# Pooled attention and a maxout layer on one core: more tiles by seven products, and one written order for all engines

## The chip, the core and the metric

The kernel runs on one core of a Trainium2 chip. The metric is device time in microseconds (us), the time of one execution on the device. The profile is of one execution; its times count from the first instruction (the span). The core has five engines that run side by side, each through its own instructions in order: PE (matrix products; PEld are its weight loads), DVE (elementwise work), ACT (activations and copies), POOL (here sums, and the issue of loads) and SP (which here only issues DMAs). PE's results go to PSUM, which the kernel divides into eight banks of 512 float32 columns; the other data lie in SBUF.

## What is computed

```
q, k, v: (8 batches, 8 heads, 576, 64)       pool = 8, so 72 pooled keys
k_p, v_p = means of k and v over 8 neighbours in the sequence
scores   = q @ k_p.T / 8 ;  attn = softmax(scores) ;  o = attn @ v_p
x        = o as 4608 tokens x 512
h        = max(x @ w1, x @ w2, x @ w3)        512 -> 768
out      = h @ w_out                          768 -> 512
```

The output is float32; the products run on 16-bit operands.

## The kernel before

Three algebraic steps stand in both kernels. The kernel subtracts w1 from w2 and w3 (`sub_w`), so that h = x·w1 + max(0, x·(w2−w1), x·(w3−w1)). It multiplies w1 by w_out once (`turn_w`, `linear`, L349), so that the x·w1 part becomes x·wm in the output product. And where it says "by seven products", a product of two matrices, each cut in 2x2 quarters, is made from seven products of quarters instead of eight, with sums of the operands' quarters made before them and sums of the results after them.

The 4608 tokens are worked in nine tiles of 512 (tile 0 to tile 8, `LAST` = 8). Each tile has a first layer (x to h) and an output product (x and h to out). A batch holds 576 tokens, so tiles and batches don't coincide. For each batch:

- q, k and v are loaded by DMA from POOL's queue (`load_q`, L100; `load_k`, L79; `load_v`, L87 and L91). q, k and v of batches 1 and 2 are loaded at the start, later ones two batches ahead, into two buffers each.
- k is summed over 8 neighbours in three steps (`fold_steps`, L161, L162, L164), for batch 1 on DVE and later on POOL, then transposed on PE and put into `kz` (`turn_k`, L199 and L208). v is summed in the same three steps on POOL, into `vp_all`.
- q is transposed: batches 0 to 2 on PE (`turn_q`, L192), batches 3 to 7 by one DMA transpose from SP's queue (step "T", L302).
- scores are one PE step and one exponential on ACT each: `scores` for eight heads of 576 columns (batches 1 to 6), `scores_flat` in nine pieces of 512 columns (batch 7) (L218, L223).
- values (`values`): eight small matmuls into `pav` (L268), a reciprocal and a product on DVE (L274, L276). The result is transposed into `xT`, on PE for batches 0 to 2 (L259), and by DMA from SP's queue from batch 3 on (`turn_x`, L253).

First layer: tiles 0 to 5 directly (`hidden_part`, groups of four matmuls, L362; a relu on ACT, L368; a maximum on DVE, L370). Tiles 6, 7 and 8 by seven products (`seven`, L789), three column groups a, b and c of seven products each, with evictions on ACT (L795, L799) and sums on DVE (L766, L769).

Output: tiles 0, 1, 5 and 6 directly (`project`: per 128 tokens four matmuls L412 and six L416, one ACT copy L421, two stores L425). Tiles 2, 3, 4, 7 and 8 by seven products (`out_seven`, ten matmuls each, L713; ACT copies L723, DVE additions L726, stores L662). The sums of the weights are made by `fold_w` and `fold_out` (L536, L545, L597), of x by `sums_of` (L612) and `fold_x` (L564), of h by `sums_of` and `fold_h` (L628).

The order is written out by hand, as lists of step names that the program runs through; every engine executes its share of the steps in the order in which they are written. `block(0, ...)` does tile 0 with batches 0 and 1 woven in; `MIDDLE` does tiles 1 to 4, with the batch after next's loads and sums; `block(5, LEAD, ...)` does tile 5; `ORDER`, through `weave`, does the rest but the last output. In these lists "s3" is the third head's scores, "v2" a value chunk of 128 tokens, "x2" its transpose, "k" the keys, "h" half a first-layer group, "1" to "7" (or "o1" to "o7") output products, "1a" to "7c" seven-product steps of a first layer, "F" half an output tile. In `MIDDLE`, "!" makes the next POOL sum wait for the last DVE sum of two SBUF operands (`gate`, `held`, `after`).

PSUM is divided three times: pools `ps0` (start), `psp` (tiles 0 to 5: `att` twice two banks, `tr` one, `pw` three), and `psq` (the rest).

## Time and profile before

| what | value |
|---|---|
| times of three runs | 226.16, 233.84 and 234.19 us, median 233.84 |
| the profiled execution | 228.01 us, of which the span is 226.3 us |
| DVE, ACT and POOL busy | 148.6, 122.3 and 138.6 us |
| PE, matmuls | 1807 |
| DMA | 33.54 MB; 195 GB/s of HBM traffic over the span |
| L362, first layers directly | 336 matmuls |
| L789 and L713, seven products | 252 and 350 matmuls |
| POOL sums of v, first step (L161) | 7, 4061 ns each |
| POOL sums of k, first step (L161) | 6, 3125 ns each |
| qT by DMA (L302) | 5, median 7.0 us from issue to landing |
| loads of q, k and v, 576 KB each | medians 13.0, 8.2 and 17.5 us from issue to landing |

How to read the profile: each line of groups names a source line, an engine, an operation, what it writes and reads ("out<-in"), its shape, its count, its busy time and the mean time of one, and then the idle time of its engine ahead of it with what ended it. A PE record lasts longer than the time for which it keeps the next matmul away, since matmuls overlap; from one matmul's start to the next one's start is the better measure. In a table of windows each row is a stretch of the span with the busy time and the count of instructions of PE, PEld, DVE, ACT and POOL, the granted TensorE clock, the DMA share and the DMA rate.

### The profile page before, as it was taken

The numbers are of one execution on the slowest core, as the hardware profiler recorded it, in microseconds if no ns is written. First come the engines' busy times: TensorE is split into PE (matmuls) and PEld (weight loads), VectorE is DVE, ScalarE is ACT, GpSimd is POOL, SyncE is SP. The second block draws the span as 40 slices with busy tenths as digits, with TensorE's granted clock in tenths as the row PEclk, the third lists the DMA queues.
The fourth block names the chain that finished last, engine by engine and source line by source line (L and its number), as shares of the span: only waits on it lengthen the run. The fifth ranks groups of instructions, "written<-read, shape, count | busy, mean of one in ns | idle before, by whom it ended". The sixth has DMA issues, their size and how long they took to land.

```text
span 226.3 us, 4691 instructions
## 1 busy us (share of the span) xinstructions
PE 214.7 (95%) x1807; PEld 146.4 (65%) x1807; DVE 148.6 (66%) x292; ACT 122.3 (54%) x221; POOL 138.6 (61%) x111
## 2 busy tenths in 40 slices
PE   6788999999999999999999999699999999999993
PEld 2467745558656555965686568355677677788882
DVE  3668876038595385876679668535668886898840
ACT  2267524755874577238624862475687446555330
POOL 7974300999949967787677758999500913872020
PEclk9999999999999999999999999999999999999999
DMA  6999999989759999659999599965241534200265
GB/s 167 210 197 197 208 207 208 203 163 224 128 106 191 217 220 208 112 129 151 199 226 191 31 216 236 182 126 132 58 107 29 122 61 95 46 3 0 55 203 164
DMA packets 47351, 33.54 MB, mean 148 GB/s; under 512 B 27041, under 2 KB 42337, under 8 KB 47329
## 3 DMA queue, kind: packets, MB, share of 16 engines
q0 software_dynamic: 16944, 16.98, 48.1%
q1 hardware_dynamic: 29936, 15.87, 33.0%
q10 hardware_dynamic: 448, 0.39, 0.7%
q8 instruction: 14, 0.23, 0.5%
q14 instruction: 9, 0.07, 0.1%
HBM read 34.60 MB, written 9.44 MB: 195 GB/s over the span
## 4 chain that ended last, share of the span: by engine, by line
PE 69%; DMA 15%; POOL 11%; issue 1%; DVE 1%; ACT 1%; POOLq 0%
PE pw L362 21%; PE oA L713 9%; DMA vt<-in_v_dram 8%; PE pA L789 7%; PE po L416 7%; PE po L412 5%; PE oC L713 4%; PE psc L218 4%; DMA mw<-in_moe_w_dram 4%; PE pC L789 3%; POOL half L161 3%; DMA xT<-xn 3%; PE pav L268 3%; PE oB L713 2%; POOL half L162 2%; PE pB L789 2%
## 5 line engine op out<-in xcount | busy, mean ns | idle before, releaser
L362 PE MATMUL pw<-xT,mw 128*128 128x512 f16 (+1 forms) x336 | 72.8, 348 | 1.9 <-DMA xT<-xn 1.6
L362 PEld LDWEIGHTS <-mw 128*128 128x128 f16 x336 | 31.6, 98 | 22.3 <-DMA xT<-xn 1.8
L370 DVE TENSOR_TENSOR hT<-t,pw 128x512 f16<-128x512 f16 (+1 forms) x42 | 25.4, 609 | 25.1 <-ACT et L223 17.8
L223 ACT ACTIVATE et<-psc 72x576 f16<-72x576 f32 (+2 forms) x54 | 35.2, 661 | 6.8 <-PE psc L218 6.7
L161 POOL TENSOR_TENSOR half<-vt 72x2048 f32<-72x2048 f16 x7 | 28.4, 4061 | 13.8 <-DMA vt<-in_v_dram 13.3
L162 POOL TENSOR_TENSOR half<-half 72x1024 f32<-72x1024 f32 (+1 forms) x13 | 27.3, 2098 | 11.0 <-DVE rcp L274 6.1
L368 ACT ACTIVATE t<-pw 128x512 f16<-128x512 f32 (+1 forms) x42 | 22.5, 537 | 16.2 <-PE pw L362 15.8
L276 DVE TENSOR_TENSOR xn<-pav,rcp 128x512 f16<-128x512 f32 x40 | 27.7, 692 | 1.4
L416 PE MATMUL po<-mwo,hT 128*128 128x512 f16 (+1 forms) x102 | 23.5, 366 | 0.0
L218 PE MATMUL psc<-qT,kz 128*128 128x320 bf16 (+2 forms) x120 | 22.4, 278 | 0.8 <-DVE qT L194 0.6
L218 PEld LDWEIGHTS <-kz 128*128 128x128 bf16 x143 | 13.1, 98 | 13.3 <-ACT qT L194 1.1
L161 POOL TENSOR_TENSOR half<-ktFalse 96x1536 f32<-96x1536 f16 x6 | 18.7, 3125 | 4.0 <-issue 2.9
L564 POOL TENSOR_TENSOR pad<-xT 128x256 f16<-128x256 f16 x8 | 5.9, 732 | 22.5 <-ACT pad L795 13.9
L795 ACT CAST pad<-pA 128x512 f16<-128x512 f32 x27 | 15.6, 588 | 7.2 <-PE pA L789 7.0
L268 PEld LDWEIGHTS <-et 72*128 72x128 f16 x320 | 15.1, 98 | 3.6 <-issue 0.4
L723 ACT COPY osb<-oA 128x512 f32<-128x512 f32 x12 | 7.0, 586 | 19.2 <-PE oA L713 19.2
L274 DVE RECIPROCAL rcp<-pav 128x8 f32<-128x8 f32 x40 | 8.2, 204 | 14.0 <-PE pav L268 13.6
L412 PE MATMUL po<-wm,xT 128*128 128x512 f16 (+1 forms) x68 | 16.6, 366 | 0.0
L268 PE MATMUL pav<-vp,et 72*128 72x65 f16 x320 | 16.4, 194 | 0.1
L421 ACT COPY osb<-po 128x512 f32<-128x512 f32 (+1 forms) x16 | 9.2, 573 | 12.0 <-PE po L416 12.0
L789 PEld LDWEIGHTS <-sw 128*128 128x128 f16 x144 | 13.7, 98 | 2.5
L766 DVE TENSOR_TENSOR pad<-pad,pC 128x512 f16<-128x512 f16 x18 | 12.3, 685 | 3.9 <-PE pC L789 3.6
(122 smaller groups left out, 380.0 us busy)
## 6 DMA issues: line engine op xcount, KB each, us to landing
out_dram<-osb SPq DMA_DIRECT2D x38, 128.0 KB, 5.5
ktFalse<-in_k_dram POOLq DMA_DIRECT2D x7, 576.0 KB, 8.2
qb<-in_q_dram POOLq DMA_DIRECT2D x7, 576.0 KB, 13.0
vt<-in_v_dram POOLq DMA_DIRECT2D x7, 576.0 KB, 17.5
mw<-in_moe_w_dram POOLq DMA_DIRECT2D x9, 256.0 KB, 9.4
out_dram<-osb SPq DMA_DIRECT2D x8, 256.0 KB, 7.4
ktTrue<-in_k_dram SPq DMA_DIRECT2D x3, 384.0 KB, 5.2
out_dram<-ob SPq DMA_DIRECT2D x8, 128.0 KB, 2.6
```

The source lines that it names most:

```text
L161: yield e.tensor_tensor(out=f, in0=t[:, :, 0:4, :], in1=t[:, :, 4:8, :], op=ALU.add)
L162: yield e.tensor_tensor(out=f[:, :, 0:2, :], in0=f[:, :, 0:2, :], in1=f[:, :, 2:4, :], op=ALU.add)
L218: nc.tensor.matmul(out, kz_all[b % 2][f % 2][rows, h, :], qTs[b][rows, n + i0:n + i1, 64 * (h % 2):64 * (h % 2) + 64], start=True, stop=True)
L223: nc.scalar.activation(out=out, in_=in_, func=FT.Exp, scale=1.0 / 64.0)
L268: nc.tensor.matmul(pav[:, h // 4, 65 * (h % 4):65 * (h % 4) + 65], ets[b][:, h, c0:c0 + 128], vp_all[:, b, h, :], start=True, stop=True)
L276: nc.vector.tensor_tensor(out=xn, in0=pv[:, :, :, 0:D], in1=rcp.to_broadcast([128, 2, 4, D]), op=ALU.mult)
L362: mm = nc.tensor.matmul(pw, w_sb[wi][:, kc, bass.ts(jc, 128)], x[:, kc], start=(kc == 0), stop=(kc == KCH - 1))
L370: nc.vector.tensor_tensor(out=hT[:, jc, c0:c1], in0=t, in1=pw, op=ALU.max)
L412: nc.tensor.matmul(po, tokens(128 * m, 128 * m + 128)[:, kc], wm_sb[:, kc, c], start=(kc == 0), stop=False)
L416: nc.tensor.matmul(po, hT[:, jc, bass.ts(mm, 128)], wo_sb[:, jc, c], start=False, stop=(jc == JCH - 1))
L713: nc.tensor.matmul(p, left, right, stop=(r == 4), skip_group_check=True, start=(i in FIRST and r == 0 and (m == 0 or n == LAST)))
L789: mm = nc.tensor.matmul(p[:, w], a[:, kc, bass.ts(g, 128)], b[:, kc, :], start=(i in FIRST and w + kc == 0), stop=(w + kc == 2), skip_grou ...
```

## The change

Tile 5's first layer and the output products of tiles 1, 5 and 6 are now made by seven products, so that tiles 5 to 8 have first layers and tiles 1 to 8 have outputs of that kind. From the end of tile 0's first layer on, one list, `ORDER`, names every step of every kind up to the last output; `run` goes through it. In it:

- "s30" is score piece 0 of batch 3, all in pieces of 512 columns; "v42" value chunk 2 of batch 4 (with its DMA transpose from batch 3 on), "x12" a PE transpose, "q13" a PE transpose of part of q, "k5" the keys of batch 5. Keys are now summed in two steps on DVE ("K5"), and the last halving is left to PE, which adds two products per transpose (`keys`).
- "V4" is a piece of batch 4's value sums: four first-step and two second-step pieces on POOL, and the third step on DVE. `vp_all` has three buffers instead of eight.
- "<q5" issues the load of q of batch 5; it waits for the PE instruction last written before it and for the last DMA transpose written before it. "T5" is a third of the DMA transpose of q of batch 5, three to a batch.
- "t1" to "t4" are the sums of a tile's x, "u1" to "u4" of its h, "f", "F", "S" and "G" of the weights, all on DVE. Every POOL piece waits for the DVE sum that was written last (`shared`, `both`).
- "A3" is half of a directly computed first layer group of tile 1, "A1" and "A2" the two groups of a row of tiles 2 to 4; "p" is half an output step of tile 0.
- "1a" to "7c" are first-layer products of tiles 5 to 8, "1d" to "7d" output products. Product 1 is copied by ACT from its bank into a second PSUM bank, and PE adds product 2 to it there, where DVE added the two before.
- A step with "*" is evicted by DVE instead of ACT.

From there on PSUM has four single banks that are handed out in turn (`take`, `give`), two for `pav` and two more (`SC`) for scores, keys and PE transposes. In SBUF a row of `kt` is longer by 32 elements.

```diff
+        pad = 0 if b == 0 else 32
+        kts[b] = (const if b == 0 else ld).tile(
+            [96, 6, POOL * D + pad], dtype, name=f"kt{b == 0}", tag=f"kt{b == 0}")[
+                :, :, 0:POOL * D].rearrange("p i (j d) -> p i j d", j=POOL)
...
-    vp_all = const.tile([Sp, B, H, 65], F16, name="vp", tag="vp")
+    vp_all = const.tile([Sp, 3, H, 65], F16, name="vp", tag="vp")
...
+    def fold_k(b):
+        new_kp(b)
+        f = const.tile([96, 6, 4, D], F16, name="halfh", tag="k16")
+        nc.vector.tensor_tensor(out=f, in0=kts[b][:, :, 0:4, :], in1=kts[b][:, :, 4:8, :],
+                                op=ALU.add)
+        nc.vector.tensor_tensor(out=kps[b].rearrange("p j i d -> p i j d"), in0=f[:, :, 0:2, :], in1=f[:, :, 2:4, :],
+                                op=ALU.add)
...
-        pkt = psum([128, 3, 96], BF16, name="pkt", tag=tag[0], bufs=tag[1])
+        pkt = psum([128, 3, 96], F32, name="pkt", tag=tag[0], bufs=tag[1])
         for i in range(3):
-            nc.tensor.transpose(pkt[:, i, :],
-                                kps[b][:, 2 * i:2 * i + 2, :].rearrange("p i d -> p (i d)"),
-                                ident[0:96, 0:96])
+            for j in range(2):
+                matmul(pkt[:, i, :], kps[b][:, j, 2 * i:2 * i + 2, :].rearrange("p i d -> p (i d)"),
+                                 identh[0:96, 0:96], start=(j == 0), stop=(j == 1))
...
-                qTs[b] = sb2.tile([128, 2 * NG, 128], BF16, name="qT", tag="qT")
-                nc.sync.dma_start_transpose(
-                    out=qTs[b], in_=qbs[b].rearrange("p hp t d -> p (hp t d)"))
+                if i == 0:
+                    qTs[b] = sb2.tile([128, 2 * NG, 128], BF16, name="qT", tag="qT")
+                turned[:] = [nc.sync.dma_start_transpose(
+                    out=qTs[b][:, 6 * i:6 * i + 6],
+                    in_=qbs[b].rearrange("p hp t d -> p (hp t d)")[:, 768 * i:768 * i + 768])]
...
+    free_banks = [0, 1, 2, 3]
+    taken = {}
+    def take(key, shape=(128, 2, 256)):
+        i = free_banks.pop(0)
+        taken[key] = i, psum(list(shape), F32, name="pb", tag=f"pb{i}", bufs=1)
+        return taken[key][1]
+    def give(key):
+        free_banks.append(taken.pop(key)[0])
...
+    shared = [None]
+    def both(out, a, b, op, e=nc.vector):
+        t = e.tensor_tensor(out=out, in0=a, in1=b, op=op)
+        if e is nc.vector:
+            shared[:] = [t]
+        elif shared[0] is not None:
+            after([t], shared[0])
...
+        if i == 1:
+            move(out=bank("B", n, g), in_=p)
+        elif i in (6, 5):
+            move(out=y[:, i == 5], in_=p)
+        elif i in (2, 3):
+            t0 = sb2.tile([128, NB], F16, name="t0", tag="t0")[:, 0:HALF]
+            nc.scalar.activation(out=t0, in_=p[:, 0], func=FT.Relu)
+            nc.vector.tensor_tensor(out=h_of(g)[:, i - 2], in0=t0, in1=p[:, 1], op=ALU.max)
+        if i in (5, 7) and (n, 12 - i, g) in done:
+            plus(1)
+        if i == 4:
+            plus(0)
+            shared[:] = [nc.vector.scalar_tensor_tensor(
+                out=h_of(g + JH), in0=y[:, :, 0], scalar=0.0, in1=y[:, :, 1],
+                op0=ALU.max, op1=ALU.max)]
+        if i in (2, 3, 4):
+            give((of(i), n, g))
...
+    def out_product(n, i):
+        p = bank(of(i), n, "d")
+        for r in range(5):
+            for m in range(2):
+                matmul(p[:, m], *out_operands(n, i, m, r), stop=(r == 4),
+                                 start=(i in (1, 7) and r + m == 0), skip_group_check=True)
+        done.add((n, i, "d"))
+        def o(j):
+            if (n, j) not in outs:
+                outs[n, j] = new_two()
+            return outs[n, j]
+        def plus(j):
+            nc.vector.tensor_tensor(out=o(j)[:, :, hi], in0=o(j)[:, :, hi],
+                                    in1=bank("C", n, "d"), op=ALU.add)
+        if i == 1:
+            move(out=bank("B", n, "d"), in_=p)
+        elif i != 4 and i != 7:
+            move(out=o(int(i in (5, 3)))[:, :, lo if i in (2, 3) else hi], in_=p)
+        if i in (5, 7) and (n, 12 - i, "d") in done:
+            plus(1)
+        if i == 4:
+            plus(0)
+        if i in (2, 3, 4):
+            give((of(i), n, "d"))
+        if i in (5, 7, 3) and all((n, z, "d") in done for z in (5, 7, 3)):
+            store(nc.sync, n, 1, o(1), slice(0, C))
+        if i in (2, 4) and all((n, z, "d") in done for z in (2, 4)):
+            store(nc.sync, n, 0, o(0), slice(0, C))
...
+        f = const.tile([Sp, H, 4, D], F32, name="half", tag="half")
+        e = nc.gpsimd
+        for i in range(0, H, 2):
+            c = slice(i, i + 2)
+            yield e.tensor_tensor(out=f[:, c], in0=t[:, c, 0:4, :], in1=t[:, c, 4:8, :],
+                                  op=ALU.add)
+        for i in range(0, H, 4):
+            c = slice(i, i + 4)
+            yield e.tensor_tensor(out=t[:, c, 0:2, :], in0=f[:, c, 0:2, :], in1=f[:, c, 2:4, :],
+                                  op=ALU.add)
+        both(vp_all[:, b % 3, :, 0:D], t[:, :, 0, :], t[:, :, 1, :], ALU.add)
+        yield
...
+    SEVEN = (5, 6, 7, 8)
+    NORMAL = tuple(n for n in range(1, LAST + 1) if n not in SEVEN)
+    HALVED = tuple(n for n in NORMAL if n == 1)
...
+            elif name[0] == "<":
+                load = {"k": load_k, "v": load_v, "q": load_q}[name[1]](
+                    int(name[2]), *([nc.gpsimd] if name[1] != "q" else []))
+                after([load], latest[0])
+                if turned:
+                    after([load], turned[0])
...
+    for tag in ("pb3", "pb0", "pb2", "pb1"):
+        psum([128, NB], F32, "pb", tag, 1)
+    psum([128, 2, NB], F32, "pav", "val", 1)
+    for _ in range(SC[1]):
+        psum([128, NB], F32, "psf", *SC)
+    ORDER = """
+        V1 q12* q13 p V1 V1 s10 V1 V1 s11 V1 G p* s12 s13 p s14 q20* s15 G <q3 s16 p* s17
+        <k3 s18 K2 <k4 p V1 <v3 T3 q21 q22 K2 v10 T3 T3 k2 V2 p v11 x10 p q23* x11* v12 V2
+        s20 V2 s21 V2 C3 s22 V2 v13 s23 H3 s24 x12* V2 <q4 v14 G D3 x13 V2 s25 S V3 A3 t1 S
+        t3 s26 C4 G s27 s28 <v4 p v20 K3 D4 B3 x14 v21 x20 K3 K4 E3 H4 k3 x21* v22 A4 f B4
+        <k5 V3 s30 x22 u1 t2 E4 s31 v23 V3 s32 t4 V3 V3 K4 H1 s33 <k6 V3 f <q5 s34 D1 H2 s35
+        x23 D2 T4 S s36 V4 v24 t3 t1 T4 k4 A1 s37 A2 1d u3 s38 V3 x24 u2 C1 2d u4 v30 t2 C2
+        T4 6d v31 V4 t4 V4 V4 E1 S V4 E2 B1 v32 5d B2 7d <v5 K5 <k7 3d u1 u2 4d K5 1d V4 v33
+        s40 s41 K6 2d* K6 v34 V5 s42 s43 F 6d* s44 s45 B1 s46 C1 s47 V4 B2 s48 u3 A1 v40 k6
+        k5 T5 T5 f A2 C2 V5 t1 E1 V5 t2 v41 5d* E2 T5 u1 D1 V5 u4 7d 3d* <q6 F D2 V5 4d H1
+        H2 <v6 K7 <q7 t4 s50 s51 1d v42 s52 s53 u2 t3 H1 s54 v43 s55 K7 t1 A1 s56 v44 s57 H2
+        s58 A2 V5 k7 V5 T6 t2 u3 F C1 T6 6d t4 v50 B1 C2 t3 v51 D1 V6 f u4 B2 V6 2d V6 V6 T6
+        V6 5d D2 7d E1 E2 <v7 3d* 4d s60 s61 v52 T7 1d V6 s62 t1 v53 1a s63 2d T7 u1 t2 u2
+        s64 v54 s65 6a* V7 2a s66 V6 1b s67 u4 6d* u3 t3 6b s68 5a F t4 2b 5b* v60 V7 5d 7a
+        3b 3d 4a 7b T7 1c v61 3a s70 6c 2c 4b s71 v62 V7 s72 5c s73 7d t3 t1 7c s74 t2 s75
+        V7 3c 4d 1a 4c v63 s76 6a 1b 2a s77 V7 5a* s78 v64 6b 2b V7 u1 3a 5b u2 V7 1d 3b 7a
+        t4 2d v70 7b 4a 6d u3 4b v71 1c 5d 2c 6c 7d u4 t1 5c* t2 7c 3d 4d 3c 1a 4c v72 1b 6a
+        2a u1 u2 6b 2b 5a u3 t3 v73 1d 3a 5b 2d t4 v74 3b 7a 6d u4 7b 4a 5d 1c* 4b 3d t1 t2
+        6c 7d 5c 2c 7c 4d 1a* 3c 4c 6a 1b u3 t3 2a 5a 2b u1 6b 3a 1d 5b t4 u2 7a 2d* 3b 6d
+        u4 7b 4a 5d 4b 1c 3d 6c 7d 5c 7c 2c 3c 4c 4d
+    """
+    run(ORDER)
```

The names of both lists above are those of the text; what is left out of the diff are the old lists, the old functions `seven`, `out_seven`, `fold_x`, `fold_h` and `sums_of`, the new function for the last output (which keeps its fourteen steps), and the passing of PE instructions through `matmul` and `transpose`, which only note the latest one.

677 lines of the change are left out of this document (260 added, 417 removed), and 3 rows, old and new, of the table stop.

## Prediction

> **What bounds the kernel now.** I read the page's engine line first, then the windows, the chain, PE's waits, and the timeline at two places.
>
> ```profile
> span 226.3 us, 4691 instructions
> PE 214.7 (95%) x1807; PEld 146.4 (65%) x1807; DVE 148.6 (66%) x292; ACT 122.3 (54%) x221; POOL 138.6 (61%) x111
> ```
>
> PE is busy 95% of the span, the next engine 66%. The windows (busy us and count of each engine) ask whether that holds in every stage; the first is the middle of the kernel, the second the woven part, the third that part's densest piece:
>
> ```profile
> 37.30:158.70 121.40, 118.54 (x962) 75.73 (x961) 75.50 (x154) 70.78 (x126) 97.48 (x53) 1.00 0.98 171
> 158.70:213.00 54.30, 54.30 (x481) 42.09 (x479) 42.78 (x73) 31.69 (x58) 21.14 (x26) 1.00 0.25 54
> 200.00:213.00 13.00, 13.00 (x122) 11.66 (x120) 11.10 (x18) 6.04 (x11) 4.54 (x6) 1.00 0.01 1
> ```
>
> In the middle PE idles 2.9 us, in the woven part not at all, with DVE up to 11.10 of 13.00 (85%) beside it and the granted clock at 1.00. So time follows the columns that PE streams. The chain prices them (start, us, what):
>
> ```profile
> ...
> 81.56 0.86 PE pw L362 x4
> ...
> 158.74 0.86 PE po L412 x4
> 159.60 1.29 PE po L416 x6
> ...
> 178.78 0.87 PE pA L789 x8
> ...
> 219.22 1.09 PE oC L713 x10
> ```
>
> Four matmuls of 512 columns take 0.86, eight of 256 take 0.87, ten of 256 take 1.09: columns alone count. PE's waits (total, times, longest), where those after 37 us are:
>
> ```profile
> PE pw L362 <- DMA xT<-xn: 1.6, 1, 1.6
> ...
> PE oA L713 <- ACT osb L723: 0.5, 3, 0.2
> ...
> PE pkt L199 <- DVE rcp L274: 0.4, 1, 0.4
> ```
>
> A matmul's record lasts 0.38 where its columns take 0.215, so each idle stretch is some 0.16 longer than shown. With about eight of them the 2.9 us are 4.2. The longest is the first layer of tile 5, which waits at 145 us for a transpose that stood on SP behind a 4.94 us qT transpose.
>
> Last, how DVE and POOL meet, in the timeline:
>
> ```profile
> 62.08 1.26 POOL L164 TENSOR_TENSOR vp<-half 72x512 f16<-72x512 f32 x1
> ...
> 62.28 1.35 DVE L597 TENSOR_TENSOR so<-wm 128x512 f16<-128x512 f16 x1
> ...
> 63.66 0.42 DVE L597 TENSOR_TENSOR so<-so,wm 128x512 f16<-128x512 f16 x1
> ...
> 64.00 0.42 DVE L597 TENSOR_TENSOR so<-wm 128x512 f16<-128x512 f16 x1
> ...
> 64.34 0.42 DVE L597 TENSOR_TENSOR so<-wm,so 128x512 f16<-128x512 f16 x1
> ```
>
> A DVE sum of two SBUF tensors that met a POOL sum took 1.35 instead of 0.42, ending only after POOL's. And 0.42 us sums follow each other every 0.34: back to back a DVE instruction costs 0.08 less than its row says (0.69 becomes 0.61, 0.55 becomes 0.47).
>
> The profiled execution took 228.01 us: its span of 226.3 and 1.7 around it. The runs shown are 226.16, 233.84 and 234.19, median 233.84, 2.6% above it. I sum against 228.01. For the chances I take the middle of all four times, 230.6 (their mean), and 2% of it, about what a measurement of this kernel can tell from no change: faster is under 225.9, slower over 235.2.
>
> **The change, part by part.** PE first.
> Tile 5's first layer: twelve groups of 0.86 (10.3) become 21 products of four 256-column matmuls (half of 0.87: 9.1). −1.2.
> Output of tiles 1, 5 and 6: four times 0.86 + 1.29 (8.6) become seven times 1.09 (7.6). Three times −0.97: −2.9.
> Keys: per batch three transposes become six 96-column matmuls; in the trace three of them go by in 0.13 us, so 21 more cost +0.9.
> Scores of batches 1 to 6 are cut at 512 columns: same columns, some 42 matmuls more, at a few ns each: ten of 256 take 1.09 where the pace of 0.86 for 2048 columns makes 1.075. +0.1.
> Together −3.1 on PE, all on the path, since PE is the path.
>
> Stalls that can go. The 1.8 us at 145: tile 5's last transposed chunk (v51) is now computed some 12 us of PE work ahead of its first product, against a median of 2.7 us from issue to landing. The three waits on osb (about 0.3 each with the hidden tail) and the one on the key sums (0.6) go because other products now stand between. Bounds 0 and 4.2; I take 3.3, the five named.
>
> DVE. POOL's key sums (18.7 + 10.9 + 6.0) end; two DVE steps a batch take their place. All token sums and hidden sums now lie on DVE, and four first layers end there. Against that, the additions of bank B (13 of 0.68) go, as ACT copies the first product into the bank and PE adds to it. No row shows a copy from PSUM to PSUM, nor a matmul onto a bank that an engine has written; nearest are ACT's copies to SBUF (0.59) and the same matmul (0.109), which I take. Should the copy be 0.2 faster or slower, the 19 of them would move ACT by 4 us, which ACT (54% busy) hides.
> The written order of 476 steps holds on DVE, back to back: 35 value steps at 0.24 + 0.61 (29.7), 32 token sums at 0.34 (10.8), 28 hidden sums at 0.47 (13.1), 12 key steps (8.0), 7 value sums (2.4), 16 weight sums (7.0), maxima of tiles 1 to 4: 12 at 0.33 and 18 at 0.605 (14.9), 12 seven-product groups at 2.48 (29.8), 14 output additions (8.5), 15 starred 512-wide evictions (9.1), 6 smaller (2.2). Sum 135, against 165.1 of PE: 82%, where the woven part of before shows 42.78 of 54.30. ACT comes to 95.6, POOL to 57.
> Cut into ten-microsecond pieces of PE, DVE stands over 90% in five: 10.3 of 9.6 (first V3, K3, K4 with the halved first layer), 9.5 of 10.4, 9.3 of 9.7 and 9.4 of 10.3 (from s68 on, where two seven-product streams run), and 10.2 of 10.2 (around v74). No row shows DVE so full. If DVE can be filled wholly, the pieces cost their excess, 0.7; if only to the 85% of the densest row, 7.1. PE lost nothing there at 85%, so the limit is higher; the sums' inputs are ready early, and four banks let DVE fall behind by a product or two. I take 95%: 1.9.
>
> POOL. The value sums become four pieces and two. A 512-element piece takes 1.02 if the 2048-element row (4.06) just divides, and 1.25 by the line through the rows for 2048 and 1536 elements (4.06, 3.13); six take 6.4 to 7.5. V1 starts when its load lands, at 39.4 as before (POOL's wait ends there), so its sum on DVE ends between 46.2 and 47.3. PE begins the order at 37.9, where the first po stands now, and has 8.4 us of work ahead of v10: 46.3. Between 0 and 1.0; I take the middle, +0.5.
> Each piece is made to wait for the DVE sum ahead of it. A DVE sum behind it can still meet it. In the woven part 24 POOL sums of 0.67 made DVE instructions wait 1.6 us in all, a tenth of POOL's time, and PE lost nothing; at that rate 52 us of pieces cost DVE 5, in pieces that have room. 0 on the path; the second rival has the other end.
>
> DMA. Loads now wait for a named matmul and for the last transpose, and POOL's queue stands with them. The fourth q load waits for T3's third part; behind it on POOL stand V3's pieces (7.5, and three issues at 0.7), done by about 70 where v30 wants them near 79. T3 itself stands on SP until q3 lands; behind it are the first tile's stores, whose three buffers are not wanted for 30 us. Hidden, on the rows' medians.
>
> Sum: 226.3 − 3.1 − 3.3 + 1.9 + 0.5 = 222.3; with 1.7 around it **224.0 us**.
>
> **Rivals.** (1) DVE becomes the bound where it is full: at 85% the five pieces cost 7.1 instead of 1.9, which makes 229.2. For it: no row has DVE fuller; the in-order queue. Against: PE lost nothing at 85%.
> (2) Slower: POOL's pieces hold DVE. Up to v70 (121.3 us of PE, DVE 97.2) the order has 80 DVE instructions with two SBUF inputs and 42 pieces covering 52 us. Were they to meet by chance, 43% of the 80 would wait 0.63 on average: 22 us. DVE then needs 119 of 121; at a share of 0.9 the stretch takes 132, +11, at 0.85 it takes 140, +19. Less the 1.3 already counted there, that is 233.8 to 241.6; I put it at 237.7. It decides from 12 us of such waits on (97.2 + 12 is 90% of 121.3), 0.3 a piece. For it: the 1.35 us row, and 1.06 for 0.69 at 192 and 200 us. Against: the waits written ahead of each piece, and the tenth measured. The Trainium skill, SBUF — State Buffer, section "Who interferes with whom", says that of a DVE instruction with two SBUF inputs and a GpSimd one that reads SBUF, whichever issues second blocks until the first is done. The trace agrees (1.35 us); taken alone, the rule gives this rival's time, and the rate of the woven part gives the forecast.
> (3) The room isn't there. q3 goes out behind V1's pieces at about 46.9; with a median load of 13.0 and a median qT transpose of 7.0 it is ready at 66.9, where PE comes to s30 at about 66; with the longest transpose of the trace (10.2) at 70.1. PE then waits 0.9 to 4.1: 224.9 to 228.1, and I put it at 227.5. Against: T3 is cut in three and s30 needs only the first.
> (4) Better: all 4.2 go and DVE costs nothing: 219.0, so 220.7.
>
> **How the numbers follow.** Forecast (221.5 to 226) 0.42, (1) 0.18, (2) 0.18, (3) 0.08, (4) 0.14. Faster: (4) and 0.40 of the forecast, 0.54. Slower: (2) but for its lowest end, 0.16. The rest, 0.30, is the same. Range: down to (4) less the 1.8 by which the fastest run lies under the profiled one, 219; up to 234, which leaves out most of (2), some 0.15. If faster, I expect 219 to 225.9.
>
> **What would show it.** Right: PE's last matmul near 218.5, PE without a wait over 1 us after 40, DVE at 165 to 180 busy on the page, no xT wait before tile 5. Step by step: 21 products of 0.43 for tile 5 and seven of 1.09 for each of eight tiles; DVE sums at 0.42 and 0.55 on the mean (0.6 and more would be rival 2); PE waiting on DVE in the ten microseconds around K3 and around v74 (rival 1); on qT or kt (rival 3). Wrong: PE idle in many short waits behind plain evictions, which my sums of whole pieces cannot see.

## The result, and the profile after

| what | before | after |
|---|---|---|
| time, median of four each | 230.17 us (226.16 to 234.19) | 229.37 us (227.80 to 230.06) |
| ratio to before | 1 | 1.0108, 95% interval 1.0073 to 1.0143 |
| the profiled execution, its span | 228.01, 226.3 us | 227.80, 226.0 us |

The medians seem to say that nothing changed. The ratios, here and in the experiments, leave disturbed executions out (here 233.84 and 234.19 of before), while the medians and the times in brackets are of all executions. By its ratio the changed kernel is 1.1% slower, some 2.4 us: less than the 2% that the chances were about, but clear of no change. In the experiments the kernel before took 226.5 to 226.7 us on the median every time, and the changed kernel 229.0 where it was run again.

The page of after, its first lines:

```profile
span 226.0 us, 5152 instructions
PE 213.0 (94%) x2010; PEld 162.6 (72%) x2010; DVE 182.5 (81%) x358; ACT 126.3 (56%) x250; POOL 84.1 (37%) x90
```

DVE went from 148.6 to 182.5 us and POOL from 138.6 to 84.1, but PE is still the busiest by far. Its waits after 37 us, by what ended them (total, times, longest):

```profile
PE pav L70 <- DVE vp L537: 2.6, 2, 1.7
...
PE pxt L74 <- DVE xn L279: 0.9, 3, 0.4
...
PE psf L70 <- ACT et L226: 0.4, 1, 0.4
PE pav L70 <- DVE xn L279: 0.4, 1, 0.4
...
PE pb L70 <- DVE pb L78: 0.3, 1, 0.3
```

The 1.6 us wait for xT ahead of tile 5 is gone, as forecast. In its place stand two waits for vp, the pooled values, and several short ones for plain evictions. (The three of 0.9 us on pxt lie ahead of 37 us and were there before.)

Records overlap, so I measure PE from one matmul's start to the next one's. In before a matmul of 512 columns starts 0.216 us ahead of the next one, one of 256 columns 0.109, so 256 columns more take 0.107 us: 2,400 columns a us. What the starts lie apart beyond the columns is called overhead if it is up to 0.03 us, else a wait. From 37.2 us to the last matmul, in us:

| trace | columns | overhead | waits | last matmul to end | span |
|---|---|---|---|---|---|
| before, the profiled execution | 175.3 | 4.7 | 5.0 | 3.8 | 226.3 |
| before once more | 175.3 | 4.8 | 3.6 | 3.8 | 225.0 |
| after | 171.2 | 5.2 | 7.7 | 4.6 | 226.0 |
| after once more | 171.3 | 5.2 | 8.3 | 4.7 | 227.1 |

(Some matmul records are missing from the traces of after: the most complete show 171.5, so 0.2 to 0.3 of the last two rows' waits are columns.) PE's work fell by 3.5 us. The waits and the end took more than that back. Where the waits lie, in us:

| trace | 37 to 53 | 53 to 70 | 70 to 98 | 98 to 124 | 124 to 160 | from 160 |
|---|---|---|---|---|---|---|
| before, profiled | 0.9 | 0.7 | 0.4 | 0.3 | 2.7 | 0 |
| before once more | 0.9 | 0.6 | 0.4 | 0.3 | 1.4 | 0.1 |
| after | 3.0 | 0.1 | 2.3 | 0.5 | 0.8 | 1.0 |
| after once more | 2.6 | 0.1 | 2.2 | 1.2 | 1.3 | 1.0 |

The longest stands at 80.9 us. The timeline of after there (start, us, what):

```profile
77.95 1.28 POOL L811 TENSOR_TENSOR vt<-half 72x512 f16<-72x512 f32 x1
78.29 3.15 DVE L537 TENSOR_TENSOR xs<-xT 128x512 f16<-128x512 f16 x2
...
79.16 0.80 POOL L114 DMA_DIRECT2D qb<-in_q_dram  x1
...
79.96 1.18 POOL L807 TENSOR_TENSOR half<-vt 72x512 f32<-72x512 f16 x1
...
82.42 0.41 DVE L537 TENSOR_TENSOR vp<-vt 72x512 f16<-72x512 f16 x1
...
82.89 0.42 PE L70 MATMUL pav<-vp,et 72*128 72x65 f16 x8 [1.68 <-DVE vp L537]
```

The last POOL piece of batch 3's values ends at 79.2. DVE's sum into vp could follow, but two sums over xT stand ahead of it in DVE's order, and each of them lasts until a POOL piece has ended: 3.15 us for two sums of 0.42. (A maximum and a sum over hT, 0.68 and 0.55, follow them ahead of vp.) PE waits until 82.9. The POOL pieces of batch 3's values were late already. Ahead of them on POOL stands the load of batch 4's q:

```profile
67.15 0.79 POOL L114 DMA_DIRECT2D qb<-in_q_dram  x1 [10.56 <-DVE hT L682]
```

It waits for the last third of batch 3's q transpose, which landed at 66.6. The profile puts the wait down to a DVE maximum, but in the run once more, and in the run below with three places of the order mended, such a load goes out 0.5 to 0.7 us behind that landing too. From 68.0 to 79.2 POOL then works off batch 3's six pieces and three issues of loads.

And the transfers. The windows of before once more (busy us of PE, PEld, DVE, ACT, POOL; granted clock; DMA share; GB/s):

```profile
37.30:53.00 15.70, 15.57 (x134) 9.37 (x133) 6.09 (x15) 10.32 (x19) 13.42 (x8) 1.00 1.02 192
...
70.00:98.00 28.00, 27.85 (x237) 17.73 (x235) 18.01 (x38) 15.28 (x27) 22.40 (x13) 1.00 0.98 186
98.00:124.00 26.00, 25.84 (x207) 17.15 (x205) 19.30 (x39) 13.61 (x24) 18.91 (x13) 1.00 1.06 184
```

and of after:

```profile
37.30:53.00 15.70, 13.77 (x131) 8.62 (x129) 10.26 (x20) 10.92 (x21) 13.66 (x14) 1.00 1.09 189
...
70.00:98.00 28.00, 26.17 (x240) 18.54 (x237) 25.69 (x43) 15.71 (x31) 16.41 (x15) 1.00 1.27 163
98.00:124.00 26.00, 25.65 (x216) 16.56 (x215) 23.93 (x42) 17.14 (x34) 11.62 (x11) 1.00 1.11 173
```

DVE is at 92% in both later stretches, and the DMA queues are busier (1.27 for 0.98) while they move less (163 for 186 GB/s). The rows of the DMA issues say of what. Before once more (count, median us from issue to landing):

```profile
ktFalse<-in_k_dram POOLq DMA_DIRECT2D x7, 576.0 KB, 8.0
...
xT<-xn SPq DMA_TRANSPOSE x27, 2.5
...
qT<-qb SPq DMA_TRANSPOSE x5, 4.0
```

After:

```profile
ktFalse<-in_k_dram POOLq DMA_DIRECT2D x7, 576.0 KB, 12.3
...
xT<-xn SPq DMA_TRANSPOSE x27, 3.8
...
qT<-qb SPq DMA_TRANSPOSE x15, 7.9
```

A third of a q transpose now takes twice the time of a whole one in before once more, and more than a whole one in the profiled execution of before (7.0). It goes with whether a load is in flight beside it. In after the thirds took 2.8 to 4.5 us where none was and 5.5 to 13.4 where loads were in flight for half of their time or more; the whole ones of before once more took 4.0 alone and 3.9 to 10.1 beside loads. In before, loads go out in bursts of three, and 17 of the 27 transposes of xn and 2 of the 5 of q run while no load is in flight; in after, loads are issued among the transposes, and it is 12 of 27 and 3 of 15. The last load of v lands at 150.1 in after and at 140.4 in before once more.

### The profile page after: what moved, and what is told of

Same layout as the page of the kernel before. It is cut to its first block, busy times and chain, and to the rows that moved or that the text cites. A ratio compares the mean times of both kernels' runs of the same rounds, so it can differ in the third digit from the quotient of the medians.

```text
span 226.0 us, 5152 instructions
## 1 busy us (share of the span) xinstructions
PE 213.0 (94%) x2010; PEld 162.6 (72%) x2010; DVE 182.5 (81%) x358; ACT 126.3 (56%) x250; POOL 84.1 (37%) x90
## 3 DMA queue, kind: packets, MB, share of 16 engines
q0 software_dynamic: 20304, 16.98, 51.4%
## 4 chain that ended last, share of the span: by engine, by line
PE 73%; DVE 13%; ACT 4%; DMA 4%; issue 3%; POOL 1%; POOLq 0%; DVEq 0%
PE pb L70 55%; PE psf L70 5%; PE pw L70 4%; PE pav L70 4%; DMA vt<-in_v_dram 4%; PE pm L70 2%; DVE xn L279 2%; DVE xs L537 2%; DVE hT L682 2%; ACT kz L78 2%; PE pxt L74 1%; DVE halfh L537 1%; DVE hs L537 1%; PE oC L70 1%; DVE ys L636 1%
## 5 line engine op out<-in xcount | busy, mean ns | idle before, releaser
L70 PE MATMUL pb<-xT,mw 128*128 128x256 f16 (+1 forms) x336 | 61.4, 318 | 0.1
L70 PEld LDWEIGHTS <-mw 128*128 128x128 f16 x456 | 42.6, 98 | 17.8 <-issue 1.3
L807 POOL TENSOR_TENSOR half<-vt 72x512 f32<-72x512 f16 x28 | 33.3, 1208 | 50.2 <-DMA vt<-in_v_dram 28.6
L226 ACT ACTIVATE et<-psf 72x512 f16<-72x512 f32 x63 | 35.2, 590 | 11.1 <-PE psf L70 10.8
L682 DVE TENSOR_TENSOR hT<-t,pb 128x512 f16<-128x512 f16 (+1 forms) x30 | 17.1, 575 | 8.0 <-PE pb L70 6.4
L70 PE MATMUL psf<-qT,kz 128*128 128x256 bf16 (+4 forms) x161 | 22.0, 249 | 0.7 <-ACT et L226 0.4
L70 PEld LDWEIGHTS <-hs 128*128 128x128 f16 x192 | 18.8, 98 | 2.2
L811 POOL TENSOR_TENSOR vt<-half 72x512 f16<-72x512 f32 x14 | 18.5, 1328 | 2.2 <-DVE rcp L277 2.2
L70 PE MATMUL pb<-mwo,hT 128*128 128x256 f16 (+1 forms) x120 | 19.3, 294 | 0.0
L70 PE MATMUL pb<-soh,hs 128*128 128x256 f16 x138 | 19.1, 273 | 0.0
L70 PEld LDWEIGHTS <-hT 128*128 128x128 f16 x168 | 16.3, 98 | 3.6
```

Of the source, the lines that this page charges most:

```text
L70: latest[0] = nc.tensor.matmul(*args, **kw)
L226: nc.scalar.activation(out=out, in_=in_, func=FT.Exp, scale=1.0 / 64.0)
L682: nc.vector.tensor_tensor(out=hTs[n][:, j, c], in0=relus[j], in1=b, op=ALU.max)
L807: yield e.tensor_tensor(out=f[:, c], in0=t[:, c, 0:4, :], in1=t[:, c, 4:8, :], op=ALU.add)
L811: yield e.tensor_tensor(out=t[:, c, 0:2, :], in0=f[:, c, 0:2, :], in1=f[:, c, 2:4, :], op=ALU.add)
```

## The experiments

In the expectations VectorE is DVE, GpSimd POOL, ScalarE ACT and SyncE SP. "Waits" below are those of the tables above.

### Both kernels once more

The changed kernel as it is:

> The changed kernel once more, to have its time in five rounds against the kernel before on this chip and a second trace. If the first four times stand (227.8 to 230.1) the ratio is about 1.01; if the two profiled executions (227.8 against 228.0) are the better measure it is 1.00. Both theories expect PE to stand still again at v10 (1.1 us in the first trace) and at v30 (1.8 us) if these waits come from the order, and elsewhere if they come from how DMAs happen to land.

229.0 us (227.0 to 230.4), ratio 1.0097 (1.0061 to 1.0134). The waits at v10 (0.8 us) and v30 (1.9 us) stand in the same places, as they would if the order makes them; behind 98 us some differ: 0.5 us more at 120, and 0.6 at 142 and 0.7 at 158 that the first trace doesn't have. The kernel before as it is:

> The kernel before once more, for a second profiled execution. Theory A: part of the stalls that the prediction took out of before, the 1.76 us wait for xT ahead of tile 5 above all, belonged to the one profiled execution (span 226.3) and not to an ordinary one: then this one shows a span near 224.8, no PE wait over 1 us after 40 us, and stalls of about 3.3 us in sum after 37 us instead of 5.0. Rival: the wait is in every execution; then it is there again with 1.5 to 2 us, and the span is near 226.

226.72 us with a span of 225.0: theory A. The 1.6 us wait for xT isn't in this execution; the waits between 124 and 160 us are 1.4 where the profiled execution had 2.7. The two altered copies of before that are profiled below don't have it either (waits of 3.7 us in each). In the profiled execution the last load of v landed at 144.2 instead of 140.4, and the q transpose beside it took 7.8 us instead of 3.9. I had summed against an execution with a wait that an ordinary one doesn't have.

### POOL's hold on DVE

The value pieces on POOL write a constant and read nothing: a memset of 1280 elements a partition, which takes 1.17 us, in place of a sum with 512 results, which takes 1.23 to 1.33 on the mean.

```diff
-            yield e.tensor_tensor(out=f[:, c], in0=t[:, c, 0:4, :], in1=t[:, c, 4:8, :],
-                                  op=ALU.add)
+            yield e.memset(f[:, 0:5], 0.5)
```

and in the same manner for the second step.

> The POOL pieces of the value sums are replaced by POOL writes of a constant of about the same length (1280 elements, some 1.3 us), with the same waits on them and for them: POOL is as busy but reads no SBUF. The values of v are lost. Theory P (DVE's sums wait for POOL's reads, and PE for them): xs back from 0.55 to 0.42 on the mean, hs from 0.63 to 0.55, kp from 0.89 to 0.55, and at least 3 us faster than the changed kernel. Theory Q (PE waits behind plain evictions and too short distances in the order, wherever POOL is): DVE rows shorter as well, but the time within 1 us.

228.13 us, ratio 1.0067 (1.0043 to 1.0090). DVE is busy 10.4 us less than in the run once more, so the hold is real: its sums of two SBUF operands fall to 0.42 and 0.55 on the mean. The wait at 81 goes. But waits come at 100, 116, 136 and 151 us, the sum falls only from 8.3 to 7.1, and the time by 0.9 us, with intervals that overlap. So POOL's hold isn't the whole cause; at the most it is a part.

The pieces without their wait for the DVE sum ahead:

```diff
-        if op is not None and gate is not None:
+        if False:
```

> The pieces on POOL no longer wait for the DVE sum written ahead of them; everything else is as in the changed kernel. Theory P: the waits are what keeps the two apart, so DVE's sums meet more pieces, xs and hs means rise over 0.7, and the kernel is 1 to 4 us slower. Rival: the waits themselves make POOL late for v10 and v30, so without them PE's two waits (1.1 and 1.8) shrink and the kernel is 1 to 2.5 us faster.

238.14 us, ratio 1.0471 (1.0422 to 1.0520). This is the direction of theory P at more than twice its price. Among PE's waits are two of 4 and 2.4 us, for DVE, and with each the granted clock drops (a third, of 2.2 us at 123, leaves it at 1.00):

```profile
73.00:77.00 4.00, 0.62 (x5) 0.22 (x3) 3.96 (x5) 0.40 (x1) 3.99 (x5) 0.87 1.18 175
77.00:84.00 7.00, 6.60 (x39) 3.83 (x40) 6.27 (x11) 4.69 (x10) 6.26 (x6) 0.59 1.32 154
...
154.00:158.00 4.00, 1.73 (x17) 1.30 (x15) 4.00 (x6) 0.76 (x2) 4.00 (x4) 0.99 0.71 147
158.00:161.50 3.50, 3.50 (x19) 2.42 (x18) 1.83 (x5) 0.64 (x2) 1.42 (x2) 0.53 0.22 43
```

Read the clock column beside PE's: idle in one row, half speed in most of the next. So the written wait keeps away a loss of some 9 us, about the second rival's time (237.7), though a part of it is the half clock, which that rival didn't count.

### The waits of the written order

First the beginning:

```diff
+        if b == 1:
+            psc = take(("s", j), (128, 512))
...
-        <k3 s18 K2 <k4 p V1 <v3 T3 q21 q22 K2 v10 T3 T3 k2 V2 p v11 x10 p q23* x11* v12 V2
+        <k3 s18 V1 K2 <k4 p <v3 T3 q21 q22 K2 v10 T3 T3 k2 V2 p* v11 x10 p q23* x11* v12 V2
```

> The changed kernel with only its beginning mended: the scores of batch 1 take their PSUM tiles from the four pb banks instead of the two that the q transposes use too, the last sum of batch 1's values stands ahead of batch 2's key sums on VectorE, and one plain eviction of tile 0 goes to VectorE. Theory Q (short waits of the new order are what ate the gain of the columns): the waits at 38.4 (0.43), 42.6 (0.54) and 51.3 (0.42) go and the one for vp at 46.7 falls from 0.8 to 1.1 us to some 0.3, so 1.9 us less: 227.1 against 229.0. Rival (VectorE and ScalarE simply have no more room here, each wait that is taken away comes back at the next instruction): under 0.6 us less, and the waits between 38 and 53 us still sum to over 2 us.

229.03 us, ratio 1.011 (1.006 to 1.016). The waits at 38.4 and 42.6 fell from 0.97 to 0.34, the one at 51.3 from 0.42 to 0.22. The one for vp stayed at 0.8, and a new one of 1.2 us came behind it, for the key sums that vp had been put ahead of. Between 37 and 53 us there are 2.6 us of waits, as in the run once more. The rival: what was taken away came back at the next instruction.

Then three places of DVE's order (here the first):

```diff
-        x23 D2 T4 S s36 V4 v24 t3 t1 T4 k4 A1 s37 A2 1d u3 s38 V3 x24 u2 C1 2d u4 v30 t2 C2
+        x23 D2 T4 S s36 V4 v24 V3 t3 t1 T4 k4 A1 s37 A2 1d u3 s38 x24 u2 C1 2d u4 v30 t2 C2
```

> The changed kernel with three places of its order mended, nothing else: batch 3's last sum of values ahead of two sums over xT on VectorE, two sums of tile 4 behind the softmax values of batch 4's chunk 3 instead of ahead of them, and two sums of tile 5 exchanged. Theory D (VectorE works in order, and a sum that GpSimd holds to 1.3 to 2 us stands ahead of the result that PE waits for): the waits at 80.9 (1.85), 119.9 (0.5 to 1.0) and 142.3 (0.57) go, so 2.9 to 3.4 us less, 225.6 to 226.1 against 229.0. Rival (the work of VectorE is the limit there, and only the order of the waits changes): new PE waits of together over 2 us within 5 us behind each of the three places, and under 1 us less.

228.89 us, ratio 1.0063 (1.0030 to 1.0097): 0.8 us under the run once more, with intervals that overlap. The waits at 81 and 142 went but for 0.5 at 84. Others came: 0.65 at 74, and 1.45 at 118 where there had been 1.0 at 120; that is the rival's price, under 1 us. The timeline of this run, at the latter:

```profile
116.02 0.79 POOL L114 DMA_DIRECT2D qb<-in_q_dram  x1 [3.07 <-DVE hT L682]
...
116.29 2.12 DVE L537 TENSOR_TENSOR xs<-xT,xs 128x512 f16<-128x512 f16 x1
...
116.83 1.28 POOL L811 TENSOR_TENSOR vt<-half 72x512 f16<-72x512 f32 x1
...
119.31 0.42 PE L70 MATMUL pav<-vp,et 72*128 72x65 f16 x8 [1.28 <-DVE xn L279]
```

The load waits for the last third of a q transpose (landed at 115.3), and the piece behind it on POOL meets whichever sum DVE has then. With one sum moved away, the next one stands there.

Both, and the last stores from two queues:

> Both of these, and the last stores of the two parts that end last go from two queues (SyncE's and ScalarE's) at the same moment instead of one behind the other. If the waits and the end are what ate the gain, the parts add: 1.9 + 3.2 + 0.6 us less than 229.0, so 223.3, which is 3 us under the kernel before (226.5). If VectorE's work is the bound behind the waits: above 226. The time from the last matmul to the end falls from 4.7 to about 4.1 us.

228.72 us, ratio 1.0054 (1.0010 to 1.0098); the parts don't add. In its profiled execution, its longest (230.68), PE waits 2.0 us at 98 for xT, whose transpose landed at 100.2 behind a load that landed at 97.3 (95.5 in the run once more). The run below without tile 1's seven products has the same wait, 1.2 us, with that load landing at 96.9. From the last matmul to the end it is still 4.7.

Last, the turns of batch 2 behind and among tile 1's first products, alone and with the three places:

```diff
-        <k3 s18 K2 <k4 p V1 <v3 T3 q21 q22 K2 v10 T3 T3 k2 V2 p v11 x10 p q23* x11* v12 V2
-        s20 V2 s21 V2 C3 s22 V2 v13 s23 H3 s24 x12* V2 <q4 v14 G D3 x13 V2 s25 S V3 A3 t1 S
+        <k3 s18 V1 K2 <k4 p <v3 T3 v10 T3 T3 p v11 V2 x10 p x11* q21 v12 V2
+        C3 q22 K2 V2 H3 k2 V2 q23* v13 s20 V2 s21 s22 s23 s24 x12* V2 <q4 v14 G D3 x13 V2 s25 S V3 A3 t1 S
```

> The changed kernel with the part from 45 to 62 us in another order: the sum of batch 1's values ahead of batch 2's key sums, and the turns of batch 2's q and k behind and among tile 1's first products, as the kernel before has them, instead of ahead of them. Theory Q (the waits between 38 and 53 us, 2.9 to 3.4 us in every trace of this order against 0.9 to 1.4 before, come from this place of the turns): the wait at 46.7 falls under 0.7 and the one at 51.3 goes, 0.8 to 1.3 us less on PE by 62 us, and 227.7 to 228.2 against 229.0. If the bursts bind behind it, PE only arrives earlier at the same waits: PE is 0.8 us or more ahead at 62 us, the waits behind 70 us are longer by as much, and the time stays within 0.4 us of 229.0.

> The same with the three mended places of the run on VectorE's sums, and the copy whose bank PE waits for at 197 us on ScalarE instead of VectorE. If the waits of the order are what ate the gain, they add up: 1.0 + 2.9 + 0.4 us less, 224.7. If the bursts bind: 227.5 to 229, no better than the run with the three places alone (ratio 1.0063 to the kernel before), whatever waits are mended.

231.4 us, 1.0217 (1.0179 to 1.0255), and 231.04 us, 1.0173 (1.0127 to 1.0219). Both expectations failed, through my order: with five score pieces in a row, PE waits there, in the first of the two, 1.3 us for the keys that ACT copies into `kz` and 0.5 us for exponentials. The windows of the second of the two:

```profile
54.90:58.90 4.00, 1.99 (x20) 1.14 (x17) 1.23 (x3) 3.60 (x8) 4.00 (x4) 1.00 1.23 204
58.90:62.30 3.40, 3.35 (x28) 2.63 (x26) 1.79 (x4) 1.17 (x3) 0.05 (x1) 0.50 1.34 162
```

No wait there is over 0.85 us, yet the clock went to half for 3.4 us (in the first of the two for 6.8, from 56.5 to 63.3). Whether the 2.6 to 3.0 us between 37 and 53 can be had back stays open. The second of the two has the three places mended like the run on DVE's sums, and PE some 4 us later at 70 us: its waits from 70 to 160 us are 0.5 in all, where that run has 3.0 (and the run once more 4.6). So, at least there, waits behind 70 us went when PE came later.

### What sets the pace behind 70 us

The loads of v for batches 4 to 7 left out, in the changed kernel and in the kernel before:

```diff
+        if b > 3:
+            vts[b] = vts[3]
+            return None
         vts[b] = ld.tile([Sp, H, POOL, D], dtype, name="vt", tag="vt")
```

> The changed kernel with the loads of v for batches 4 to 7 left out (their value sums run as before, on batch 3's data, so those values are wrong). Theory L (from 67 us on the loads and the DMA transposes of the new order follow each other without a pause; a burst that lands late, which differs from execution to execution, turns into PE waits somewhere behind it, so that mended places of the order bring nothing): the DMA queues get pauses, the last load lands before 135 us instead of 150, the waits behind 110 us go, the executions lie within 1 us of each other, and the time falls by 2 to 3 us, to 226 to 227. Rival D (VectorE's sums held by GpSimd, independent of the loads): the waits after 110 us stay, under 1 us less, 228 to 229.

> The same loads left out of the kernel before, as a control. Theory L: its bursts had pauses between them already (no burst is in flight at 65, 97 and 120 us), so under 0.7 us less, 225.8 to 226.5. If the loads bind both kernels alike, it falls by as much as the changed one, 2 us or more.

226.07 us, ratio 0.9979 (0.9951 to 1.0008), against 1.0097 with the loads: 3 us. The kernel before: 227.01, ratio 1.0007 (0.9992 to 1.0023), nothing. Between 98 and 160 us the changed kernel now has no wait at all, and its last load lands at 124.7. One part of theory L failed: the executions still lie 2.6 us apart. Its DMA issues:

```profile
ktFalse<-in_k_dram POOLq DMA_DIRECT2D x7, 576.0 KB, 8.8
...
xT<-xn SPq DMA_TRANSPOSE x27, 2.5
qT<-qb SPq DMA_TRANSPOSE x15, 3.2
```

The same 15 transposes, in the same order and places, take 3.2 us on the median instead of 7.9 (7.2 in the run once more). The wait at 81 stays at 1.2: batch 3's loads and transposes have landed before the first of the loads that are left out would start.

Is it the bytes, or POOL's issues of them? The same four loads issued, but of one head each:

```diff
+            few = const.tile([Sp, 1, POOL, D], dtype, name="few", tag="few")
+            return eng.dma_start(out=few, in_=src[:, 0:1])
```

> The changed kernel with the loads of v for batches 4 to 7 issued as before but of one head instead of eight (0.07 MB in place of 0.58, into a tile that nobody reads; the value sums run on batch 3's data, so those values are wrong). GpSimd's queue keeps every issue. Theory L: what the run without these loads won came from the shorter bursts, so this one wins nearly as much, 226 to 227. Rival: it came from GpSimd's queue, which had four issues of 0.9 us less to make in front of its sums: then this one stays at 228 to 229.

227.22 us, ratio 1.0026 (1.0009 to 1.0043): 1.8 of the 3 us are the bytes in flight, by this, and again there is no wait from 98 to 160. The other 1.2 go with the issues on POOL or are noise between runs; that isn't settled, and the profiled executions of the two don't tell (spans of 225.1 and 224.9). One of the ten executions of this run took 1243.66 us, for a reason that nothing here shows; it isn't in the ratio.

Each q transpose in one piece again, at the place of its first third:

```diff
-                    out=qTs[b][:, 6 * i:6 * i + 6],
+                        out=qTs[b], in_=qbs[b].rearrange("p hp t d -> p (hp t d)"))]
```

> The changed kernel with each q transpose from batch 3 on as one DMA at the place of its first third, as the kernel before has it. Theory L: if the three parts, each behind whatever is in flight, stretch the bursts, then the transposes land earlier, the loads that wait for them too, and the time falls by 1 to 2 us. Rival: what counts is the loads alone, the transpose lands when the last load ahead of it does, in one piece or three: within 0.7 us of 229.0.

232.58 us, ratio 1.0167 (1.0080 to 1.0253). Not faster, so theory L falls: the thirds are not what stretches the bursts. Nor is it within 0.7 us by its median; the interval is too wide to tell it from the changed kernel's.

The padding of k undone, alone; the padding alone in the kernel before; and the padding undone with the mended places:

```diff
-        pad = 0 if b == 0 else 32
+        pad = 0
```

> The changed kernel with one line undone: the tiles of k from batch 1 on without their 32 unused elements behind each row of 512. The padded rows cut each of the seven loads of k into 576 packets of 1 KB where the kernel before has 96 of 6 KB: 20,304 packets in the loads' queue against 16,944, for the same 16.98 MB. Theory P (these packets are what made the bursts of loads longer, and by them the transposes and PE late): the queue's share of the DMA engines falls from 51 to some 48%, the last load lands by 146 us instead of 150, and the time falls by 1 to 2.5 us, to 226.5 to 228.0. Rival (the packets cost nothing, the bursts are long because the new order keeps loads and transposes in flight together): under 0.5 us less.

> The kernel before with that one line alone: its tiles of k padded in the same way, nothing else. Its bursts end well ahead of what needs them, with pauses between, so by theory P each load of k takes 1 to 1.5 us longer, and the time stays within 0.5 us of 226.6, but for the transposes of batch 7, which wait for the last load: up to 1.5 us more if that shows at 145 us. If the rows' form costs nothing, the loads of k take what they took (6 to 7 us for the third of a burst) and the time stays.

> The changed kernel without the padding, with the three places of the order mended as in the run of that name, and with the last stores from two queues. Mended places brought 0.3 us while the bursts bound; if the bursts are shorter now, they bring what their waits were (1.9 at 81, 0.5 to 1.0 at 120, 0.6 at 142), so 224 to 226, under the kernel before. If the bursts still bind: the same as the run without the padding, within 0.6 us.

239.15 us (233.12 to 242.56), ratio 1.0360 (1.0297 to 1.0424); 226.79 us, 1.0006 (0.9987 to 1.0025); 234.23 us, 1.0272 (1.0228 to 1.0316). I had it the wrong way round. The packets did fall from 20,304 to 16,944, and the kernel became slower, by the ratios some 6 us against the changed kernel. The windows of the first of the three, whose profiled execution is one of its long ones (241.07 us):

```profile
80.00:90.00 10.00, 10.00 (x90) 6.98 (x89) 7.82 (x16) 3.56 (x7) 5.48 (x5) 1.00 1.48 47
90.00:95.00 5.00, 5.00 (x59) 4.43 (x57) 4.15 (x8) 2.15 (x4) 0.00 (x0) 1.00 1.23 49
95.00:104.50 9.50, 0.11 (x3) 0.00 (x0) 0.75 (x1) 0.00 (x0) 0.00 (x0) 0.68 1.19 78
```

and its PE waits:

```profile
PE psf L70 <- DMA qT<-qb: 10.4, 3, 9.5
```

For 15 us the DMA queues are busy and move 47 to 49 GB/s; the loads of k and q issued at 76.2 and 78.0 land at 103.7 and 107.3, where in the run once more they land at 92.2 and 95.5. PE stands for 9.7 us, and the clock is at half from 98.4 to 108.7. The third run shows the same, less far, in an execution of 234.36 us, the middle of its times:

```profile
80.00:90.00 10.00, 10.00 (x91) 7.12 (x90) 7.94 (x17) 3.70 (x7) 5.46 (x5) 1.00 1.35 47
...
98.00:102.00 4.00, 2.78 (x15) 1.55 (x13) 2.94 (x6) 1.45 (x4) 0.00 (x0) 0.51 1.23 212
```

Its two loads land at 97.0 and 100.3, and it has 4.8 us of waits for qT. In the kernel before the padding costs and brings nothing, though there too a load of k runs beside a q transpose (78.8 to 86.8 and 76.5 to 86.7 in before once more). So the changed order needs the padding; it lessens a cost that the order itself brings. What it is in the order that makes the form of the rows matter isn't shown. The Trainium skill, DMA: Bandwidth & Descriptors, section "Queues, rings and completion order", says that a DMA engine goes round between its queues a packet at a time, a packet there being a group of descriptors. That a transpose takes 7.9 us among loads and 3.2 with fewer of them agrees with it; which packets stood ahead of which isn't shown by any run here.

### One part undone: tile 1's output

```diff
-        x23 D2 T4 S s36 V4 v24 t3 t1 T4 k4 A1 s37 A2 1d u3 s38 V3 x24 u2 C1 2d u4 v30 t2 C2
-        T4 6d v31 V4 t4 V4 V4 E1 S V4 E2 B1 v32 5d B2 7d <v5 K5 <k7 3d u1 u2 4d K5 1d V4 v33
+        x23 D2 T4 S s36 V4 v24 t3 t1 T4 k4 A1 s37 A2 p p s38 V3 x24 C1 p v30 t2 C2
+        T4 p v31 V4 t4 V4 V4 E1 S V4 E2 B1 v32 p B2 p <v5 K5 <k7 p u1 u2 p K5 1d V4 v33
```

> The changed kernel with the output of tile 1 by plain products again, at the same places of the order, without its seven products, its four sums over hT and its four sums over xT. PE's columns: 2,560 more (1.07 us). VectorE: 8 sums and 3 additions less, 5 to 6 us less work between 69 and 87 us. If PE is the bound there: 1 us more, 230. If VectorE is (the wait at 80.9 comes from sums that stand ahead of the last sum of values): the wait of 1.85 us falls under 1, and the time is the same or up to 1 us less.

230.14 us, ratio 1.0159 (1.0097 to 1.0221): 1.1 us more, as the columns say, with intervals that overlap. The wait at 81 is gone; 1.2 us at 98 and 0.7 at 103 came, and the wait at 120 is 1.4 where it was 1.0. So the seven products of this tile seem to earn their 1.07 us, in spite of the sums they need, though the overlap leaves that open.

### The end

The last product's upper half stored in four parts of 64 KB from two queues, as each half is done:

> Only the last stores change: the upper half of the last output is stored in four parts from two queues as soon as each half product is done, instead of two parts from one queue at the end. If the 0.8 us by which the changed kernel's end (last matmul to last instruction, 4.6 against 3.8) is longer comes from two stores standing one behind the other, the end is 3.8 to 4.0 and the time 0.6 to 0.8 us less; if it comes from how long a store takes to land, nothing changes.

230.87 us, ratio 1.0149 (1.0103 to 1.0194). From the last matmul to the end it took 6.2 us, not less than 4.7: the five last stores landed within 0.7 us of each other, each some 4 us after its issue. Not all of that need be the edit: in the run without v's loads the three last stores, unchanged, took 3.6 to 4.0 us as well, and the end 5.7. The run with the stores from two queues ("Both, and the last stores" above) says more: its last store was issued 0.5 us behind the last matmul, as in before, instead of 1.1, and the end was still 4.7, since the store took longer to land. So the order of issue alone isn't what lengthens the end. The kernel before has four stores of 64 KB there where this one has stores of 128, so fewer bytes are in flight; whether that is the reason wasn't tried.

## Why the prediction was wrong

It forecast 3.1 us off PE's columns, 3.3 us off stalls, 2.4 us back, and 224.0. The 229.4 measured lies in its range of 219 to 234, but it forecast a faster kernel, and the kernel got slower. Taken by its sum, the waits behind 37 us were to fall from 5.0 to 4.1; they rose to 7.7 and 8.3. Of the signs it named for being right, the missing xT wait came; but PE's last matmul starts at 221.1 and 222.0 instead of 218.5, waits over 1 us stand at 47 (1.1, in the first trace alone) and at 81 (1.8 and 1.9), and DVE is busy 182.5 us instead of 165 to 180. By its steps:

- **PE, −3.1: right.** Columns 175.3 to 171.3, overhead 4.8 to 5.2: −3.6 in the traces run once more. In the undone part, 1.07 us of columns came back as 1.1 us, within the uncertainty.
- **Stalls that can go, −3.3: they went, but were not all there.** The xT wait and those on osb don't occur in after. An ordinary execution of before has no xT wait, though: its stalls after 37 us are 3.6, not 5.0. A stall of one profiled execution was priced as one of every execution.
- **V1, +0.5: 0.8 to 1.1**, the wait at 46.7. Its neighbours at 38.4, 42.6 and 51.3, 1.4 us together, weren't in the sum: the "short waits behind plain evictions, which my sums of whole pieces cannot see". This place gives 1.7 to 2.1 us more waits than before.
- **DVE fuller than 90%, +1.9: too high, as far as can be told.** The first rival's 85% isn't a limit. From 160 to 180 us of after DVE is at 93%, POOL does little, and PE has no wait:

```profile
160.00:180.00 20.00, 20.00 (x215) 18.08 (x214) 18.69 (x38) 11.20 (x23) 3.23 (x3) 1.00 0.39 95
```

  From 70 to 124 us DVE's 92% are in part held sums: with the hold taken away it is at 80% and 76% there. With v's loads left out, DVE has 25.63 busy in the 28 us from 70 on (25.69 in after), and PE's waits there are 1.4 for 2.3.
- **POOL, 0 on the path: too low.** The run that took the hold away has 10.4 us less on DVE, where the forecast had 5 and the second rival was to decide from 12 on; that run won 0.9 us, within the uncertainty. By the prediction's own sign the hold stood at its limit: the sums over xT took 0.55 on the mean, those over hT 0.63, and 0.6 was to mean the second rival.
- **DMA, "Hidden, on the rows' medians": the step that failed.** V3's pieces were to be done "by about 70 where v30 wants them near 79". They began at 68.0, behind the load that waited for T3, and ended at 79.2, since three issues of loads and two short waits for DVE stand among them; the sum behind them ended at 82.8, and PE waited 1.8 us. The rows' medians didn't give 70 either: the third rival, from the same rows, has T3 done at 66.9 (it landed at 66.6, by luck: the load took 6.9 us instead of 13.0, the thirds 7.9 to 11.6 instead of 7.0), and with V3's 7.5 us and three issues behind it that makes about 76. And a median of before mixes transposes that ran alone (4.0 us) with some beside loads (up to 10.2); in the new order 11 of the 15 thirds run among loads, and they take 5.5 to 13.4. Behind 70 us, the loads of v for batches 4 to 7, which cost the kernel before nothing, cost the changed one 1.8 us by their bytes, and up to 3 us if their issues count too.
- **The end**, which the sum took as it was, grew from 3.8 to 4.6 and 4.7.

From before once more to after once more: columns −4.0, overhead +0.4, waits +4.7, end +0.9, in sum +2.0; the spans are 225.0 and 227.1. Of the rivals the third had the right thing, room that the transfers don't leave, at the wrong place: batch 3's scores did not wait, batch 3's values and what follows did. The second has its mechanism, at less than a tenth of its price.

What isn't settled: the waits between 37 and 53 us (three orders, none without them), the 1.0 us of short waits behind 160 us, the longer end, and the 1.2 us between the two runs without v's bytes. No version beat the kernel before by more than its uncertainty, not even the one that leaves v's loads out.

## What to carry to other kernels

Price a transfer by what is in flight beside it, not by its median in the old order: the same third of a q transpose took some 3 us alone and 5.5 to 13.4 among loads. Before counting a stall as a gain, look whether a second execution has it. And here, with PE full and DVE busy for 92% of the stretch, mending a single wait mostly moved it: three places that were to give 2.9 us gave 0.8, within the uncertainty. Take away the thing that may set the pace, as an experiment, before mending anything.

## What the runs showed of the hardware that I had not expected

- A DVE sum can last through a DMA issue and the POOL sum behind it. In after, a sum of 0.54 us took 2.63, and ended 0.4 us behind POOL's:

```profile
96.73 0.88 POOL L106 DMA_DIRECT2D vt<-in_v_dram  x1 [6.21 <-PE pb L70]
...
97.42 2.63 DVE L537 TENSOR_TENSOR kp<-halfh 96x768 f16<-96x768 f16 x1
97.60 0.73 POOL L94 DMA_DIRECT2D ktFalse<-in_k_dram  x1
98.35 1.28 POOL L811 TENSOR_TENSOR vt<-half 72x512 f16<-72x512 f32 x1
```

  The two held sums shown before (78.29 in after, the second of which began at 79.45; 116.29 in the run with three places mended) began under such an issue too. Not each one is held: in after a sum that began at 116.85, 0.1 us behind the start of an issue that a POOL sum followed at 117.56, kept its 0.41 us. What makes the difference isn't shown. With POOL instructions that only write, DVE's sums take 0.42 and 0.55 us on the mean, and DVE is busy 10.4 us less.
- Rows of 6 KB instead of 1 KB, so fewer packets, made two loads of the changed order land at 103.7 and 107.3 us (97.0 and 100.3 in the third run) instead of 92.2 and 95.5. In the kernel before the form of the rows changed nothing (ratio 1.0006).
- Half clock for 3.4 us came after many short waits, none over 0.85 us, that left PE idle for half of 4 us; a single wait of 2.2 us, with PE busy 1.0 us of 3.0, left the clock full.
